# Moving the first batch's small work inside its periods: squares, narrowing of w_in, low part of x, hops of the sums

## The chip, the cores and the metric

The kernel runs on one core of one Trainium2 chip, as a single launch. The metric is device time in microseconds (us); smaller is better. Three runs of the kernel before gave 1159.63, 1160.09 and 1160.9 us, so its median is 1160.09 us.

## The reference

Three stages follow one another. Attention: q, k, v are 4 batches x 12 heads x 448 rows x 64; q and k are divided by the root mean square of their rows, then softmax and the product with v. An MLP on the 1792 tokens of 768 features. A mixture of 8 experts with a fixed capacity of 224 tokens each.

```
q_n, k_n = rmsnorm(q, g_q), rmsnorm(k, g_k)          # x / sqrt(mean(x*x) + 1e-6) * g
scores = q_n @ k_n.T / 8;  attn = softmax(scores);  x = attn @ v
h = x @ w_in;  g = h * clip(h + 3, 0, 6) / 6;  x = g @ w_out      # 768 -> 2048 -> 768
logits = x @ w_gate          # greedy assignment, largest logits first, 224 tokens per expert
out[mask_e] = relu(x[mask_e] @ w1[e]) @ w2[e]
```

w_in and w_out arrive as 64-bit floats, seen as pairs of 32-bit words; the kernel narrows them to 32-bit floats itself.

## The kernel before

Attention works on pairs of heads: pair i has two heads of one batch, six pairs make a batch, 24 pairs in all. For each pair: `load` (L229) brings q and k (224 KB each); `squares` (L251, ScalarE, "ACT") squares them; for pairs 2 to 9 `fold` (L256, GpSimd, "POOL") adds halves of the squares; `sums` (L267, VectorE, "DVE") reduces them; `guess` (L271, L272, DVE) makes a first value of the inverse root; `invert` refines it in three Newton steps (12 small instructions, L279 to L282, on POOL for pairs 1 to 9); `norm` (L298, POOL) multiplies q and k by it into xn; `transp` (L315) transposes xn on TensorE ("PE"), and L324 (ACT) and L327 (DVE) split the result into a high and a low part, qh, ql, kh, kl. `s1` (L338) makes scores, whose maxima DVE takes (mx, L341); `mt` (L347) transposes the maxima, and L349 (DVE) makes mr of them. `sT` (L360) makes the transposed scores less their maxima, ACT takes the exponentials (ph, L371). `pv` (L449) multiplies by v and L452 (ACT) copies the result into xn_t, of which there are two buffers. `psums` (L460 or L465) adds up the exponentials.

The sums then take a way through DRAM, called the hops here: `rs_out` (L471) stores them, `rs_in` (L476) loads them in another shape (rs), `rec` (L482, L483, DVE) takes the reciprocal (rr), `r_out` (L487) stores it, `r_in` (L493) loads it spread over the partitions (rb). `xmul` (L497, POOL) multiplies xn_t by rb, and `xsplit` makes the high part xh (L507, ACT) and the low part xl (L505, POOL). xl is the last reader of an xn_t buffer.

Beside this runs the narrowing of w_in, 16 units: a load of 768 KB (wraw, L159), one ACT and three DVE instructions (cv, L141 to L144) and a store of 384 KB (L174). From the end of the first batch the MLP of the batch that is done (h, L559) fills PE between the pieces of attention. Its weights w are loaded from the narrowed ones (win_v, L181), split by ACT and POOL or DVE (L118, L119) into one of three buffers, and stored for later batches (w_hl, L545, 768 KB).

All engines follow an order written out by hand. Each step of pair i has a due time on a scale on which a pair takes 16 units: `at(t + T, fn, i)`, with t = 16 i. The events are sorted by due time and each instruction is put at the end of its engine's queue; no engine takes one ahead of another. SyncE ("SP") issues all these DMAs in one such queue: a hop that waits for the DMA before it holds up everything behind it.

Of the kernel before, what the change touches and what calls it, by code (L numbers as in the profile page):

```python
# [21 lines left out]
def kernel(  # L22
# [45 lines left out]
    CI, CI0, CI1, CI2, CO = 6, 1.75, 2.5, 0.5, 1.5  # L68

    T_LOAD, T_VLOAD, T_NORM, T_Q, T_K, T_V = -72, -12, -38, -30, -28, 6  # L70
    T_SUMS, T_INV, T_INV0, NG0 = -50, -42, -35.5, 10
    T_S1, T_MT = (-24, -23.9, -16, -15.9), -9
    T_ST = (0, 0.1, 8, 8.1)
    T_AV = ((17, 18, 19.5, 20.5), (22, 23, 24.5, 25.5))
    T_NUM, T_XT, T_MLP = 28, 33, (37, 41, 41, 37)
    T_ADD, T_PV, T_SUM = (6, 13), (15.6, 15.62, 15.64, 15.66), 15.7
    T_RS, T_RL, T_REC, T_RO, T_RB, T_X, T_XH, T_XL = 19.5, 21.5, 24, 25.5, 28, 33, 35.5, 39.5
    GD, WD2, C_ST = 12, 8, 5
    TX0 = (20, 23, 27, 29, 32.5, 39, 42, 46)
    QMAJOR = (NP - 1, B * NP - 1)  # L80
    T_CI, D_CI, T_CO, D_CO, T_CL = 20, 10, 180, 12, 14


    order = ExitStack()
# [652 lines left out]
    def at(t, fn, *args):  # L737
        events.append((t, len(events), fn, args))
# [6 lines left out]

    for i in range(NH // 2):
        t = 16 * i
        at(t + T_LOAD, load, i)
        at(t + T_VLOAD, vload, i)
        g = GROUP[i]  # L750
        first = 16 * g[0]
        t_sq = first + T_SUMS + 4 * (i - g[0])
        at(t_sq, squares, i)
        if 2 <= i < NG0:
            at(t_sq + 2, fold, i)
            t_sq += 3
        at(t_sq, sums, i)
        late_g = 4 <= g[0] < NG0
        if i == g[-1]:
            at(t_sq if 2 <= i < NG0 else first + T_INV, guess, g)  # L760
            at(first + (T_INV0 if late_g else T_INV), invert, g)
        at(t + (T_INV0 + 0.1 if late_g and i == g[0] else T_NORM), norm, i)
        at(t + T_Q, transp, i, 0)
        at(t + T_K, transp, i, 1)
        at(t + T_V, vsplit, i)
        for c in range(NCH):
            at(t + (T_S1[c] if i else -24 + 0.1 * c), s1, i, c)
            at(t + (T_ST[c] if i else (-9, -8.9, 1, 1.1)[c]), sT, i, c)
            if i in QMAJOR:
                for s in range(2):  # L770
                    at(t + T_AV[s][c], av, i, s, c)
            else:
                at(t + T_PV[c], pv, i, c)
        at(t + (T_MT if i else -21), mt, i)
        if i in QMAJOR:
            at(t + T_NUM, normalize, i)
            at(t + T_XT, xt, i)
        else:
            for n in range(2 if i >= NP else 0):
                at(t + T_ADD[n], padd, i, n)  # L780
            at(t + T_SUM, psums, i)
            tx = TX0 if i < NP else (T_RS, T_RL, T_REC, T_RO, T_RB, T_X, T_XH, T_XL)
            for d, fn in zip(tx, (rs_out, rs_in, rec, r_out, r_in, xmul)):
                at(t + d, fn, i)
            at(t + tx[6], xsplit, i, False)
            at(t + tx[7], xsplit, i, True)
        if (i + 1) % NP == 0:
            at(t + T_MLP[i // NP], mlp_next, i // NP)
# [1 line left out]
    at(8 * H + 2, prefetch, 0)  # L790
    at(8 * H + 14, prefetch)
    for u in range(NF if wide else 0):
        for out_, t in ((0, T_CI + D_CI * u), (1, T_CO + D_CO * u)):
            at(t - T_CL, conv, (out_, u), -1)
            for part in (0, 1, 2, 3, C_ST):
                at(t + part, conv, (out_, u), part)
# [446 lines left out]
    for pi, (t, hfs) in enumerate(passes):  # L1243
# [10 lines left out]
        for f in range(NF):  # L1254
            i, k = divmod(f, QF)
# [139 lines left out]
```

## Time and profile before

| | |
|---|---|
| median of three runs | 1160.09 us |
| profiled execution: time, span of the core | 1162.06 us, 1160.2 us |
| PE busy | 1099.2 us, 95% of the span |
| DVE busy | 692.2 us, 60% |
| ACT busy | 521.3 us, 45% |
| POOL busy | 464.6 us, 40% |
| DMA | 232.17 MB, mean 200 GB/s |

The span runs from the first to the last instruction; 1.86 us of the profiled time lie outside it. The page cuts the span into 40 slices of 29 us. PE is at nine tenths or more in nearly all of them; the slices below that are mainly the first seven, and the granted clock of PE (full is 2.4 GHz, the other level 1.2 GHz) is below full mainly in slices 3, 4 and 6. A "period" in what follows is the time from one transpose of the maxima (PE t L347, one in each pair) to the next. In the first batch one takes between 12 and 20 us.

### The profile page before, as it was taken

Reading aid. Unit: us, or ns where it says so; the run is one execution under the profiler, and the core shown is the slowest. Engines: PE = TensorE matmul, PEld = TensorE weight load, DVE = VectorE, ACT = ScalarE, POOL = GpSimd, SP = SyncE. Lnnn points to the kernel's source line nnn. Section 1 sums busy time; section 2 is a strip of 40 time slices with the busy share of each in tenths; the row PEclk is TensorE's granted clock in tenths of the full one; section 3 lists DMA queues with packets and bytes.
Section 4 is the critical chain, followed back from the end, with each engine's and each line's share of the span. In section 5 each row is a group of like instructions: output and inputs, shape, how many; then the busy total and the mean of one; then the engine's idle time right before and its main releaser. Section 6 shows DMA issues by size and latency. Waiting matters only on the chain.

```text
span 1160.2 us, 19232 instructions
## 1 busy us (share of the span) xinstructions
PE 1099.2 (95%) x7073; PEld 880.7 (76%) x7073; DVE 692.2 (60%) x1440; ACT 521.3 (45%) x941; POOL 464.6 (40%) x410
## 2 busy tenths in 40 slices
PE   4978899999999999999999999999997999999997
PEld 3446556766766667787767888888887899999997
DVE  7877877886677845212341666666665846555550
ACT  4655555745545556533542111111114766666551
POOL 4665555664445533112444000000004677775540
PEclk9987989999999999999999999999998999999999
DMA  4575998978777887659996222222237888877731
GB/s 133 145 197 148 248 300 252 309 238 297 251 250 253 257 288 239 222 190 276 356 310 204 78 69 82 64 76 71 70 104 185 245 262 247 248 227 217 226 130 39
DMA packets 215357, 232.17 MB, mean 200 GB/s; under 512 B 28296, under 2 KB 188384, under 8 KB 215264
## 3 DMA queue, kind: packets, MB, share of 16 engines
q1 hardware_dynamic: 211936, 219.94, 61.6%
q0 software_dynamic: 3328, 11.01, 3.1%
q8 instruction: 55, 0.90, 0.3%
q14 instruction: 38, 0.31, 0.1%
HBM read 179.82 MB, written 51.09 MB: 199 GB/s over the span
## 4 chain that ended last, share of the span: by engine, by line
PE 67%; DVE 10%; DMA 9%; issue 5%; POOL 4%; ACT 3%; SPq 1%; POOLq 0%; DVEq 0%; ACTq 0%
PE y L1195 19%; PE h L559 15%; PE y L1347 8%; PE h L1283 5%; PE st L360 4%; PE av L449 4%; PE h L1285 3%; DMA w_hl<-w 2%; DMA we_s<-in_moe_w_dram 2%; DVE mx L341 2%; PE rt L988 1%; PE lg L601 1%; PE sm L465 1%; DMA gr<-g_dr 1%; DVE cv L143 1%
## 5 line engine op out<-in xcount | busy, mean ns | idle before, releaser
L559 PE MATMUL h<-xh,w 128*128 128x448 f32 x768 | 239.9, 382 | 1.0 <-DVE mx L341 0.5
L559 PEld LDWEIGHTS h<-xh,w 128*128 128x128 f32 x768 | 143.3, 191 | 35.9 <-issue 22.1
L559 PE MATMUL h<-xl,w 128*128 128x448 f32 x384 | 145.7, 379 | 0.0
L341 DVE TENSOR_REDUCE mx<-s 112x1 f32<-112x448 f32 x192 | 105.9, 611 | 51.6 <-PE s L338 51.3
L1133 ACT ACTIVATE g2h<-gr 128x512 fp32r<-128x512 f32 x60 | 37.9, 631 | 206.1 <-PE y L1195 161.6
L1195 PE MATMUL y<-woh,g2l 128*128 128x512 f32 (+1 forms) x448 | 124.8, 344 | 1.0 <-POOL g2l L1098 1.0
L1195 PE MATMUL y<-woh,g2h 128*128 128x512 f32 (+1 forms) x448 | 125.3, 345 | 0.0
L1195 PE MATMUL y<-wol,g2h 128*128 128x512 f32 (+1 forms) x448 | 125.2, 344 | 0.0
L1098 POOL TENSOR_TENSOR g2l<-gr,g2h 128x512 fp32r<-128x512 f32 x14 | 19.0, 1361 | 240.6 <-DMA gr<-g_dr 209.0
L119 POOL TENSOR_TENSOR wel<-we_s,weh 128x768 fp32r<-128x768 f32 x48 | 96.3, 2010 | 45.4 <-ACT weh L118 37.0
L118 ACT ACTIVATE weh<-we_s 128x768 fp32r<-128x768 f32 x107 | 88.4, 841 | 57.9 <-DMA we_s<-in_moe_w_dram 39.3
L119 DVE TENSOR_TENSOR wel<-we_s,weh 128x768 fp32r<-128x768 f32 x59 | 78.3, 1334 | 60.3 <-ACT weh L118 53.6
L371 ACT ACTIVATE ph<-st 112x448 f32<-112x448 f32 x192 | 93.0, 545 | 40.8 <-PE st L360 39.7
L442 POOL TENSOR_TENSOR pa<-ph 112x448 f32<-112x448 f32 x68 | 85.6, 1279 | 44.2 <-ACT ph L371 44.2
L1283 PE MATMUL h<-xe,weh 128*128 128x448 f32 x318 | 100.4, 375 | 2.0 <-DVE xe L1234 2.0
L559 PEld LDWEIGHTS h<-xl,w 128*128 128x128 f32 x384 | 73.2, 191 | 11.9 <-issue 7.0
L1195 PEld LDWEIGHTS y<-woh,g2l 128*128 128x128 f32 x448 | 72.0, 189 | 10.7 <-POOL g2l L1098 1.3
L1195 PEld LDWEIGHTS y<-woh,g2h 128*128 128x128 f32 x448 | 71.9, 189 | 10.6 <-issue 1.5
L1195 PEld LDWEIGHTS y<-wol,g2h 128*128 128x128 f32 x448 | 71.9, 189 | 9.1 <-issue 0.7
L1285 PE MATMUL h<-xe,wel 128*128 128x224 f32 x318 | 76.6, 268 | 0.0
L562 ACT ACTIVATE r<-h,half 128x448 f32<-128x448 f32 x64 | 40.6, 634 | 77.7 <-PE h L559 67.3
L497 POOL TENSOR_TENSOR xn_t<-xn_t,rb 128x448 f32<-128x448 f32 x22 | 25.8, 1175 | 119.7 <-DMA rb<-rec_dr 119.7
(252 smaller groups left out, 2386.1 us busy)
## 6 DMA issues: line engine op xcount, KB each, us to landing
we_s<-in_moe_w_dram SPq DMA_DIRECT2D x128, 384.0 KB
w<-w_hl SPq DMA_DIRECT2D x32, 768.0 KB
gr<-g_dr SPq DMA_DIRECT2D x52, 256.0 KB
wraw<-in_moe_w_in_dram SPq DMA_DIRECT2D x16, 768.0 KB
win_v<-w SPq DMA_DIRECT2D x32, 384.0 KB
w_hl<-w SPq DMA_DIRECT2D x16, 768.0 KB
wraw<-in_moe_w_out_dram SPq DMA_DIRECT2D x16, 768.0 KB
g_dr<-g SPq DMA_DIRECT2D x48, 224.0 KB
```

The lines of the kernel that those rows point to most:

```text
L118: nc.scalar.activation(hi, raw, AF.Copy)
L119: eng.tensor_tensor(lo, raw, hi.bitcast(F32), op=OP.subtract)
L341: mx = nc.vector.tensor_reduce(MX[i][:, s, c:c + 1], pp[s][:CP, :S], axis=AX.X, op=OP.max)
L360: nc.tensor.matmul(pp[s][:CP, :S], a[r], b[r], start=(n == 0), stop=(n == len(todo) - 1))
L371: nc.scalar.activation(e, pp[s][:CP, :S], AF.Exp)
L442: nc.gpsimd.tensor_tensor(PA[i, s, n], PP[i, s, 2 * n][0], PP[i, s, 2 * n + 1][0], op=OP.add)
L449: nc.tensor.matmul(p[r, :S], vvs[i % 2][:, s, c, V0:V0 + 64], PP[i, s, c][0], start=(c == 0), stop=(c == NCH - 1))
L559: nc.tensor.matmul(p[:, :S], lhs[:, c], x[:, c], start=(n == 0), stop=(n == 3 * NC - 1))
L1195: nc.tensor.matmul(pp[hf][:, :COLS[hf].stop - COLS[hf].start], a[:, f % QF], w[:, COLS[hf]], start=(f == 0 and n == 0), stop=(f == NF - 1 ...
L1283: mm = [lambda: nc.tensor.matmul(p[:, :4 * CP], wh[:, fo], x.rearrange("d k t -> d (k t)"), start=(c == 0), stop=(c == NC - 1), skip_group ...
L1285: lambda: nc.tensor.matmul(p[:, :2 * CP], wl[:, fo], x[:, 0], start=False, stop=False, skip_group_check=True)]
L1347: nc.tensor.matmul(p[:CP, :HW], a[:, f, tk], w[:, o], start=(f == 0 and n == 0), stop=(f == FB - 1 and n == 2))
```

## The change

Only due times change, for the first batch mostly. The squares of pairs 4 to 9 come one pair in each period, behind kh, instead of two in every other period. Their sums and folds go with them. The narrowing of w_in comes at hand-picked times, one unit in each odd period and two in each even one, behind the first four maxima; before it came every 10 units of due time whatever stood there. Its stores come 8.5 behind its start instead of 5, its loads 12.5 ahead instead of 14 (both also for w_out). The q and k loads of pairs 4 and up come 4 later. In the hops of the first batch the store of the sums comes 1.5 earlier, the load and the reciprocal 0.5 earlier, the load of rb 0.5 later, the multiplication 1.3 later, and the low part 2 earlier.

```diff
-    T_SUMS, T_INV, T_INV0, NG0 = -50, -42, -35.5, 10
+    T_SUMS, T_SQ, T_INV, T_INV0, NG0 = -50, -58.9, -42, -35.5, 10
-    GD, WD2, C_ST = 12, 8, 5
-    TX0 = (20, 23, 27, 29, 32.5, 39, 42, 46)
+    GD, WD2, C_ST = 12, 8, 8.5
+    TX0 = (18.5, 22.5, 26.5, 28.5, 33, 40.3, 42, 44)
-    T_CI, D_CI, T_CO, D_CO, T_CL = 20, 10, 180, 12, 14
+    T_CO, D_CO, T_CL = 180, 12, 12.5
+    T_CI = [16 * i + t for i in range(1, 11) for t in ((8.3, 12.3) if i % 2 == 0 or i > 6 else (8.3,))]
...
-        at(t + T_LOAD, load, i)
+        at(t + (T_LOAD if i < 4 else -68), load, i)
...
-        t_sq = first + T_SUMS + 4 * (i - g[0])
+        late_g = 4 <= g[0] < NG0
+        t_sq = t + T_SQ if late_g else first + T_SUMS + 4 * (i - g[0])
...
-        for out_, t in ((0, T_CI + D_CI * u), (1, T_CO + D_CO * u)):
+        for out_, t in ((0, T_CI[u]), (1, T_CO + D_CO * u)):
```

The change adds one line near the top, so that a line of the kernel before stands one lower in the changed one.

On DVE, around the end of the fourth period (q and k of pair 7), the kernel before has:

```order
L142 TENSOR_SCALAR cv<-cv 128x768
L327 SCALAR_TENSOR_TENSOR ql<-t,gq_72,qh 128x448
L143 SCALAR_TENSOR_TENSOR cv<-wraw,cv 128x768
L144 SCALAR_TENSOR_TENSOR cv<-wraw,cv 128x768
L327 SCALAR_TENSOR_TENSOR kl<-t,gk,kh 128x448
L267 TENSOR_REDUCE st_2_1240<-sq 112x8 x2
L271 TENSOR_SCALAR st_2_1240<-st_2_1240 112x32
L272 TENSOR_SCALAR st_2_1241<-st_2_1240 112x32
L349 TENSOR_TENSOR mr<-t,place 128x448
```

At the same place the changed kernel has:

```order
L145 SCALAR_TENSOR_TENSOR cv<-wraw,cv 128x768
L342 TENSOR_REDUCE mx_128<-s_1211 112x1
L342 TENSOR_REDUCE mx_128<-s_1212 112x1
L342 TENSOR_REDUCE mx_128<-s_1231 112x1
L342 TENSOR_REDUCE mx_128<-s_1232 112x1
L328 SCALAR_TENSOR_TENSOR ql<-t,gq_72,qh 128x448
L328 SCALAR_TENSOR_TENSOR kl<-t,gk,kh 128x448
L350 TENSOR_TENSOR mr<-t,place 128x448
```

Nothing stands between ql, kl and mr any more; the narrowing has gone ahead of the last four maxima of the period.

On ACT, at the same pair's high parts, the kernel before has:

```order
L141 ACTIVATE cv<-wraw 128x768
L371 ACTIVATE ph<-st 112x448 x2
L324 ACTIVATE qh<-t,gq_72 128x448
L251 ACTIVATE sq<-ld_q 112x512
L251 ACTIVATE sq<-ld_k 112x512
L324 ACTIVATE kh<-t,gk 128x448
```

and the changed kernel:

```order
L372 ACTIVATE ph<-st 112x448 x4
L325 ACTIVATE qh<-t,gq_72 128x448
L325 ACTIVATE kh<-t,gk 128x448
L252 ACTIVATE sq<-ld_q 112x512
L252 ACTIVATE sq<-ld_k 112x512
```

The squares have gone behind kh.

On POOL, in the third period, the kernel before has the multiplication, the first Newton step of pairs 6 and 7, then (eleven steps on) xn of pair 6 and the low part:

```order
L497 TENSOR_TENSOR xn_t<-xn_t,rb 128x448
L279 TENSOR_TENSOR st_2_885<-st_2_884 112x32
...
L298 TENSOR_TENSOR xn_998<-ld_q,st_2_884 112x2x4x64
L298 TENSOR_TENSOR xn_1000<-ld_k,st_2_884 112x2x4x64
L505 TENSOR_TENSOR xl<-xn_t,xh 128x448
```

and the changed kernel:

```order
L498 TENSOR_TENSOR xn_t<-xn_t,rb 128x448
L506 TENSOR_TENSOR xl<-xn_t,xh 128x448
L280 TENSOR_TENSOR st_2_787<-st_2_786 112x32
...
L299 TENSOR_TENSOR xn_996<-ld_q,st_2_786 112x2x4x64
L299 TENSOR_TENSOR xn_998<-ld_k,st_2_786 112x2x4x64
```

The low part has gone ahead of the twelve Newton instructions and of xn.

## Rows read from the trace of the kernel before

**Rows 1.** Busy time by period: stretch, length, PE, PEld, DVE, ACT, POOL, clock, DMA, GB/s.

```profile
37.53:51.19 13.66, 11.37 (x81) 5.82 (x81) 11.88 (x25) 10.27 (x20) 8.31 (x16) 1.00 0.43 123
51.19:64.42 13.23, 11.39 (x82) 6.04 (x82) 11.88 (x18) 7.59 (x16) 6.66 (x6) 1.00 0.71 185
64.42:82.90 18.48, 14.24 (x81) 7.02 (x82) 12.74 (x25) 8.68 (x17) 11.49 (x19) 0.82 0.72 198
82.90:95.27 12.37, 12.00 (x83) 6.42 (x81) 9.31 (x17) 9.70 (x19) 5.78 (x6) 0.86 0.73 211
95.27:115.43 20.16, 16.97 (x98) 14.07 (x98) 15.79 (x26) 9.90 (x19) 11.78 (x20) 0.72 0.46 124
115.43:135.59 20.16, 17.85 (x104) 10.77 (x104) 15.77 (x24) 12.11 (x24) 10.24 (x8) 0.86 0.96 244
157.87:184.56 26.69, 23.29 (x120) 15.92 (x118) 19.58 (x28) 12.99 (x24) 12.27 (x9) 0.87 0.96 300
```

**Rows 2.** Timeline of ACT, third period: start, length, what, idle before and releaser.

```profile
80.41 0.54 ACT L452 ACTIVATE xn_t<-av 128x448 f32<-128x448 f32 x1 [7.31 <-POOL xl L505]
```

**Rows 3.** Timeline of POOL, third period.

```profile
69.93 1.77 POOL L497 TENSOR_TENSOR xn_t<-xn_t,rb 128x448 f32<-128x448 f32 x1 [3.10 <-DMA rb<-rec_dr]
71.67 0.23 POOL L279 TENSOR_TENSOR st<-st 112x32 f32<-112x32 f32 x1
...
79.25 1.13 POOL L505 TENSOR_TENSOR xl<-xn_t,xh 128x448 fp32r<-128x448 f32 x1
```

**Rows 4.** Timeline of DVE, fifth period.

```profile
99.44 0.67 DVE L327 SCALAR_TENSOR_TENSOR kl<-t,gk,kh 128x448 fp32r<-128x448 f32 x1
...
101.60 0.18 DVE L272 TENSOR_SCALAR st<-st 112x32 int32<-112x32 int32 x1
...
108.59 0.28 DVE L482 TENSOR_TENSOR rr<-rs 112x8 f32<-112x8 f32 x1 [4.16 <-DMA rs<-sum_dr]
```

**Rows 5.** Timeline of PE: fifth and sixth period, and one wait later on.

```profile
111.02 4.61 PE L400 MATMUL av<-vv,ph 112*112 112x66 f32 x24
...
127.08 2.79 PE L465 MATMUL sm<-pa,ones 112*32 112x448 f32 x4 [2.16 <-POOL pa L442]
...
162.82 0.71 PE L360 MATMUL st<-qh,kh 64*112 64x448 f32 x1 [2.68 <-DVE g L564]
```

**Rows 6.** Groups of DVE instructions, 37.53 to 115.43: busy us, mean ns | idle before.

```profile
L143 DVE SCALAR_TENSOR_TENSOR cv<-wraw,cv 128x768 int32<-128x768 int32 x8 | 10.7, 1334 | 0.1
L144 DVE SCALAR_TENSOR_TENSOR cv<-wraw,cv 128x768 int32<-128x768 int32 x8 | 8.4, 1049 | 0.1
L142 DVE TENSOR_SCALAR cv<-cv 128x768 int32<-128x768 int32 x8 | 5.1, 640 | 1.1 <-ACT cv L141 1.1
```

**Rows 7.** Timeline of POOL: first period's Newton steps, fifth period's, the sixth's multiplication.

```profile
41.38 0.48 POOL L279 TENSOR_TENSOR st<-st 112x32 f32<-112x32 f32 x1 [1.43 <-DVE st L272]
...
46.59 0.54 POOL L282 TENSOR_TENSOR st<-st,st 112x32 f32<-112x32 f32 x1
...
101.86 0.24 POOL L279 TENSOR_TENSOR st<-st 112x32 f32<-112x32 f32 x1 [0.33 <-DVE st L272]
...
105.72 1.04 POOL L298 TENSOR_TENSOR xn<-ld_q,st 112x512 f32<-112x512 f32 x1
...
121.77 1.13 POOL L497 TENSOR_TENSOR xn_t<-xn_t,rb 128x448 f32<-128x448 f32 x1 [10.43 <-DMA rb<-rec_dr]
```

**Rows 8.** SP's queue: loads of rb for pairs 7 and 17, first and last of six.

```profile
173.73 1.11 SPq L493 DMA_DIRECT2D rb<-rec_dr  x2
...
387.04 1.10 SPq L493 DMA_DIRECT2D rb<-rec_dr  x2
```

**Rows 9.** Timeline of ACT: squares of q of pairs 13 and 23.

```profile
182.15 0.63 ACT L251 ACTIVATE sq<-ld_q 112x512 f32<-112x512 f32 x1
...
394.42 0.62 ACT L251 ACTIVATE sq<-ld_q 112x512 f32<-112x512 f32 x1
```

**Rows 10.** Chain of waits: the longest transfer it holds from 140 to 260.

```profile
241.20 9.68 DMA w_hl<-w
```

More of the change, by code (lines that the diff above doesn't have):

```diff
@@ L757 @@
         at(t_sq, sums, i)
-        late_g = 4 <= g[0] < NG0
         if i == g[-1]:
```

## The prediction

> **What bounds the kernel now.** I read the page's slices first: PE is busy 95% of the span, and where it is not, and where its clock is below full, is mainly the first 180 us. So I cut the first batch into periods, from one transpose of the maxima to the next, and read busy time and granted clock of each [rows 1]. From 51 to 136 us these take 13.23, 18.48, 12.37, 20.16 and 20.16 us (the second to the sixth; the first took 13.66). PE is idle for 1.8, 4.2, 0.4, 3.2 and 2.3 us in them, and the clock is 0.82, 0.86, 0.72 and 0.86 of full in the last four. There are only two levels, 1.2 and 2.4 GHz, so 0.72 over 20.16 us means 11.3 us at the lower one, which costs up to 5.6 us in that period. The drops come behind waits.
>
> Then I looked for what PE waits for. In the third period ACT stood 7.31 us ahead of the copy into xn_t, until POOL had made the low part xl of an earlier pair, the last reader of that buffer [rows 2]. POOL had its multiplication from 69.93 on, then the Newton steps of the next two pairs from 71.67, then their xn, and xl only at 79.25 [rows 3]: 9.3 us from the start of the multiplication to xl, most of it work of other pairs. In the fifth period DVE has a whole narrowing between ql and kl: kl comes at 99.44, the guess at 101.60, 6.3 us into the period; then it waits 4.16 us for the sums, until 108.59 [rows 4]. Behind that late reciprocal rb is late too, and POOL stands 10.43 us in the sixth period [rows 7], for which PE waits 2.16 us with the sums of the exponentials [rows 5]. These are stages in which short waits on several engines in turn set the pace, and not PE.
>
> **The change part by part.** No instruction is added or taken away; they change places. I go by periods, in the profiled execution's time.
>
> *First and second period.* The first has no late part of x in it; I take no change. In the second, DVE now has two narrowings. One is 1.33 + 1.05 + 0.64 = 3.0 us [rows 6]. DVE's busy time in the first five periods is 61.6 us, of which eight narrowings are 24.2; the rest is 7.5 us a period. So a period with one narrowing needs 10.5 us of DVE and one with two needs 13.5. The second took 13.23: +0.3. The fourth took 12.37, with 9.31 us of DVE [rows 1]: +1.1. Here DVE becomes the bound, since the last four maxima now stand behind both narrowings. At best the instructions overlap a little and both stay as they are (0); at worst the reciprocal ahead of the second narrowing waits for its sums as it did in the fifth period, 4.16 us each (+8).
>
> *Third period.* The low part goes ahead of the Newton steps, so the copy into xn_t no longer waits for them. What is late next is the Newton steps themselves, and xn behind them, which PE's transposes of the next pair need. The guess comes 6.3 us into a period as before [rows 4] (four maxima are put ahead of it, a narrowing is taken from there). xl takes 1.13 [rows 3], part of it beside the wait for the guess: Newton starts at 6.8. The twelve steps took 3.9 us beside maxima only (101.86 to 105.72), and 5.75 beside a narrowing (41.38 to 47.13), where a single step took 0.48 instead of 0.24 [rows 7]. Now a narrowing follows the guess, so I take 5, the nearer to the second: 11.8. Two xn of 1.04 each: 13.9, and half a microsecond for the last transposes (an estimate): 14.4 against 18.48, -4.1. Ends: 12.4, as the fourth period has it now, is -6.1; no gain at all is 0, where rb lands as late as now.
>
> The Trainium skill (SBUF — State Buffer, Who interferes with whom) has a rule that speaks against this place: a DVE instruction with two SBUF inputs, or in a 2-port mode, and a GpSimd instruction that reads SBUF lock each other out, and the second waits for the whole of the first. By it the Newton steps would be longer by all three narrowing instructions, 3.9 + 3.0 = 6.9, and the gain of each of the two periods 1.9 us less; the trace's 5.75 shows less than that.
>
> *Fifth period.* ql, kl and mr follow each other with nothing between, and kh is no longer behind the squares. The reciprocal no longer stands behind a load of 768 KB issued between the store of the sums and their load. What is late next is again xn, at 13.9. Behind its transposes stand 24 small products that took 4.61 us at the low clock [rows 5]; at full speed half. So 13.9 + 0.5 + 2.3 to 4.6 is 16.7 to 19; I take 17, as the waits ahead of the clock's fall are gone: -3.2. Ends: 0, and PE's busy 16.97 less the 5.6 of the clock plus 3.2 of idle time, 14.6, -5.6.
>
> *Sixth period.* With the reciprocal some 6 us earlier in the fifth, rb lands that much earlier and of POOL's 10.43 us most goes: PE's 2.16 us go, and some of the clock's loss (0.86 over 20.16 is 5.6 us at the low level, 2.8 us): -3. Ends: -5 and 0.
>
> *The later loads and stores.* By the start of the MLP's first unit one unit of w_in less has been loaded and stored: 1152 KB come into a stretch that already moves 300 GB/s with the DMA at 0.96 [rows 1], 3.8 us of transfer. PE is idle there for 3.4 us of 26.69, so part of this shows: +2, from 0 to +4. All later stages keep their order on PE, so I cost them at nothing; what hides the later q and k loads is the time between their issue and their squares (third rival).
>
> Sum: 0.3 + 1.1 - 4.1 - 3.2 - 3 + 2 = -6.9 us. The profiled execution took 1162.06 us (span 1160.2 and 1.86 around it), and would take 1155.2; it lies 2 us above the median of 1160.09. The same difference from the median gives 1153. With the ends of the likely terms, -6.1 to 0 and so on, this case has a range of its own of 1148 to 1157.5.
>
> **The rivals.** *The clock stays up.* If no wait of the new order is long enough to lower it, all the low-clock time of the third to sixth period (3.3, 1.7, 5.6 and 2.8 us of loss) goes and the idle time of the third and fifth with it: about -14, 1146. For it: each fall follows waits that the change removes. Against: PE still waits for xn in odd periods and for the maxima in even ones.
>
> *The hops stay late, and the weights' stretch takes the rest.* rb still lands late, since the multiplication is ahead of xl and the Newton steps on POOL, and the two narrowings hold up the reciprocal. The third and fifth period then gain some 2 us each, the fourth loses 1.1, the sixth gains nothing, and 2 to 4 us go to the transfers: -0.5, 1159.6. For it: 3.10 and 10.43 us of waiting for rb [rows 3, 7]. Against: the load of rs now goes ahead of wraw, and there is more time for each hop.
>
> *Slower: late q and k in the later batches.* The loads of pairs 13, 15 to 23 move behind the load of rb. Their squares stand between qh and kh on ACT. From the issue of rb's end to the squares are 182.15 - 174.84 = 7.3 us for pair 13 and 394.42 - 388.14 = 6.3 for pair 23 [rows 8, 9], six pairs of this kind. If q and k land as late as the slowest weight store here, 9.68 us [rows 10], squares and kh are 2.4 to 3.4 us late. With about 1.3 us of slack behind kh (an estimate) PE waits for 1.1 to 2.1 us in each, some 9 us, and if half of these waits lower the clock as the one of 2.68 us at 162.82 did [rows 5] (0.87 over 26.69 us is 3.5 us of loss [rows 1]), another 10: -7 + 19 = +12, 1172; it outweighs the gain from a landing of about 8.5 us on. For it: the DMA is at 0.96 in the stretch of pair 13 [rows 1]. Against: q and k together are 448 KB, little more than half of that store.
>
> **How the numbers follow.** The forecast has 0.56, the clock that stays up 0.17, late hops 0.15, late q and k 0.12. A measurement of this kernel can tell about 0.2% from no change, 2.3 us, so faster is below 1157.8. The first case gives 0.53 of its chance to faster and 0.03 to no change, the second all to faster, late hops 0.04 to faster, 0.09 to no change and 0.02 to slower: 0.74 faster, 0.12 no change, 0.14 slower. The range reaches down past the second case's 1146 and up to the late hops with somewhat more transfer time: 1145 to 1162.
>
> **What would show it.** Right: third and fifth period near 14.4 and 17 us; no wait of ACT for xl over 2 us; Newton steps the last thing ahead of PE's transposes; even periods of 13 to 14 us with the maxima as PE's releaser; POOL's 10.43 us mostly gone; all later stretches of the same length within some us. Wrong: if POOL still waits for rb in the third and fifth period by over 3 us; if PE waits for kh in the later batches, or ACT's squares for ld_q; or if the stretch from the first MLP unit to 235 us is longer by more than 4 us.

## The result, and the profile after

The changed kernel takes 1175.26 us (median of four runs, 1173.16 to 1178.29), the kernel before beside it 1160.49 us: a ratio of 1.0118, 95% interval 1.0076 to 1.016. It is slower by some 14 us. The profiled execution of the changed kernel is the longest of its four, 1178.29 us with a span of 1176.5 us.

Busy time by period after the change, where [rows 1] stood (stretch, length, then PE, PEld, DVE, ACT, POOL, clock, DMA share, GB/s):

```profile
40.72:54.07 13.35, 10.64 (x82) 5.79 (x82) 9.89 (x21) 8.44 (x17) 8.14 (x16) 1.00 0.69 184
54.07:68.05 13.98, 11.96 (x84) 6.70 (x82) 12.71 (x22) 10.33 (x19) 5.87 (x6) 0.88 0.37 104
68.05:84.72 16.67, 12.86 (x81) 7.54 (x82) 11.50 (x21) 8.44 (x16) 9.90 (x18) 0.81 0.89 236
84.72:98.91 14.19, 12.18 (x83) 6.84 (x81) 12.73 (x22) 10.30 (x19) 5.77 (x6) 0.86 0.38 105
98.91:121.64 22.73, 15.63 (x97) 14.09 (x98) 12.13 (x23) 8.76 (x17) 14.35 (x23) 0.65 0.88 232
121.64:141.60 19.96, 17.34 (x104) 10.65 (x104) 16.91 (x22) 12.13 (x23) 9.41 (x6) 0.89 0.53 134
```

Against before the first to sixth period are -0.31, +0.75, -1.81, +1.82, +2.57 and -0.20 us; ahead of the first 3.2 us are lost, from 141.6 to 457 us another 8.4, and 1.9 after that. That is 16.3 us, the difference of the two spans. In the fifth period PE is idle for 7.1 us and its clock is 0.65.

PE's waits in the changed kernel (start, length, what, idle before and releaser), the first ahead of the first period, then those at the ends of the second, third and fourth, all of the fifth with what followed, and two in the sixth:

```profile
30.71 4.87 PE L450 MATMUL av<-ph,vv 112*64 112x448 f32 x16 [0.89 <-ACT vv L305]
...
68.05 0.35 PE L348 MATMUL t<-ident,mx 112*128 112x112 f32 x1 [2.02 <-DVE mx L342]
82.92 2.01 PE L316 MATMUL t<-ident,xn 112*128 112x112 f32 x8 [3.81 <-POOL xn L299]
98.91 0.45 PE L348 MATMUL t<-ident,mx 112*128 112x112 f32 x1 [2.01 <-DVE mx L342]
...
107.77 2.04 PE L401 MATMUL av<-vv,ph 112*112 112x66 f32 x16 [2.63 <-ACT ph L372]
114.27 1.01 PE L316 MATMUL t<-ident,xn 112*128 112x112 f32 x4 [4.46 <-POOL xn L299]
115.07 1.63 PE L401 MATMUL av<-vv,ph 112*112 112x66 f32 x8
116.49 0.95 PE L316 MATMUL t<-ident,xn 112*128 112x112 f32 x4
117.24 4.61 PE L401 MATMUL av<-vv,ph 112*112 112x66 f32 x24
121.64 0.39 PE L348 MATMUL t<-ident,mx 112*128 112x112 f32 x1
...
133.58 0.94 PE L466 MATMUL sm<-pa,ones 112*32 112x448 f32 x2 [1.69 <-POOL pa L443]
135.46 0.94 PE L466 MATMUL sm<-pa,ones 112*32 112x448 f32 x2 [0.94 <-POOL pa L443]
```

The even periods wait for the maxima, as forecast; the odd ones wait for xn, and from the first xn in the fifth to its end 7.4 us pass. The other wait of the fifth, 2.63 us for ph, has the same origin as the late xn: on ACT these exponentials stand behind xh, and xh waits for rb and the multiplication.

POOL in the fifth period, where [rows 7] stood, and its next two waits:

```profile
105.22 1.45 POOL L498 TENSOR_TENSOR xn_t<-xn_t,rb 128x448 f32<-128x448 f32 x1 [2.79 <-DMA rb<-rec_dr]
107.36 1.13 POOL L506 TENSOR_TENSOR xl<-xn_t,xh 128x448 fp32r<-128x448 f32 x1 [0.69 <-ACT xh L508]
108.45 0.24 POOL L280 TENSOR_TENSOR st<-st 112x32 f32<-112x32 f32 x1
108.77 0.25 POOL L281 TENSOR_TENSOR st<-st,st 112x32 f32<-112x32 f32 x1
109.11 1.08 POOL L282 TENSOR_SCALAR st<-st 112x32 f32<-112x32 f32 x1
...
113.17 1.04 POOL L299 TENSOR_TENSOR xn<-ld_q,st 112x512 f32<-112x512 f32 x1
...
119.21 1.13 POOL L498 TENSOR_TENSOR xn_t<-xn_t,rb 128x448 f32<-128x448 f32 x1 [1.82 <-DMA rb<-rec_dr]
...
129.21 1.91 POOL L506 TENSOR_TENSOR xl<-xn_t,xh 128x448 fp32r<-128x448 f32 x1 [6.86 <-ACT xh L508]
```

DVE in the same period, where [rows 4] stood:

```profile
105.04 0.18 DVE L273 TENSOR_SCALAR st<-st 112x32 int32<-112x32 int32 x1
...
108.89 0.17 DVE L483 TENSOR_TENSOR rr<-rs 112x8 f32<-112x8 f32 x1 [1.40 <-DMA rs<-sum_dr]
...
109.21 0.91 DVE L145 SCALAR_TENSOR_TENSOR cv<-wraw,cv 128x768 int32<-128x768 int32 x1
```

The guess is 6.1 us into the period, as forecast (6.3). But the Newton steps begin at 9.5, behind rb, the multiplication, ACT's xh and xl.

In the later batches the squares [rows 9] now wait for q on ACT at two pairs, 13 and 17, and what that does shows on DVE and PE. First ACT and PE at pair 13, then ACT, DVE, POOL and PE at pair 17:

```profile
191.14 0.63 ACT L252 ACTIVATE sq<-ld_q 112x512 f32<-112x512 f32 x1 [2.16 <-DMA ld_q<-in_q_dram]
194.41 0.46 PE L339 MATMUL s<-kh,qh 64*112 64x448 f32 x2 [1.25 <-ACT kh L325]
...
279.47 0.63 ACT L252 ACTIVATE sq<-ld_q 112x512 f32<-112x512 f32 x1 [0.99 <-DMA ld_q<-in_q_dram]
...
280.14 1.28 DVE L268 TENSOR_REDUCE st<-sq 112x8 f32<-112x512 f32 x2 [0.94 <-ACT sq L252]
...
282.14 1.16 POOL L506 TENSOR_TENSOR xl<-xn_t,xh 128x448 fp32r<-128x448 f32 x1
282.30 1.03 DVE L272 TENSOR_SCALAR st<-st 112x32 f32<-112x32 f32 x1
...
286.17 0.47 PE L560 MATMUL h<-xh,w 128*128 128x448 f32 x1 [2.05 <-DVE mr L350]
```

SP's queue ahead of pair 17, which answers [rows 8]: the load of rb, then q, 7.75 us before its squares could start.

```profile
269.45 2.23 SPq L494 DMA_DIRECT2D rb<-rec_dr  x2
271.72 0.66 SPq L230 DMA_DIRECT2D ld_q<-in_q_dram  x1
```

In the kernel before, the same load was issued ahead of the store of the reciprocal, 3.4 us into its period; now it is issued 12.4 us into it, 9.0 us later:

```profile
251.78 0.46 SPq L229 DMA_DIRECT2D ld_q<-in_q_dram  x1
```

The stretch that follows (same columns as the first table; the kernel before first) is 3.45 us longer, with the clock at 0.93 instead of 1.00:

```profile
271.46:292.81 21.35, 21.24 (x128) 15.27 (x127) 13.89 (x32) 10.77 (x20) 10.22 (x10) 1.00 0.79 257
280.91:305.71 24.80, 22.75 (x127) 16.61 (x126) 15.15 (x33) 11.72 (x22) 12.13 (x12) 0.93 0.84 277
```

### The profile page after: what moved, and what is told of

The parts are those of the page before. It is cut to its first block, busy times and chain, and to the rows that moved or that the text cites. A ratio compares the mean times of both kernels' runs of the same rounds, so it can differ in the third digit from the quotient of the medians.

```text
span 1176.5 us, 19196 instructions
## 1 busy us (share of the span) xinstructions
PE 1101.2 (94%) x7073; PEld 885.3 (75%) x7073; DVE 689.9 (59%) x1440; ACT 522.0 (44%) x941; POOL 461.6 (39%) x410
## 4 chain that ended last, share of the span: by engine, by line
PE 65%; DMA 11%; DVE 11%; issue 5%; ACT 3%; POOL 2%; SPq 2%; POOLq 0%; DVEq 0%; ACTq 0%
PE y L1196 19%; PE h L560 14%; PE y L1348 8%; PE h L1284 5%; PE av L450 4%; PE st L361 3%; PE h L1286 3%; DMA sum_dr<-rb 2%; DMA rec_dr<-rr 2%; DVE mx L342 1%; DMA we_s<-in_moe_w_dram 1%; PE rt L989 1%; PE lg L602 1%; DMA gr<-g_dr 1%; DVE cv L144 1%
## 5 line engine op out<-in xcount | busy, mean ns | idle before, releaser
L1196 PEld LDWEIGHTS y<-woh,g2h 128*128 128x128 f32 x448 | 72.0, 189 | 10.6 <-issue 1.5
L450 PE MATMUL av<-ph,vv 112*64 112x448 f32 x352 | 72.7, 556 | 1.0 <-ACT vv L305 0.9
```

The costliest lines, as they stand in the source:

```text
L450: nc.tensor.matmul(p[r, :S], vvs[i % 2][:, s, c, V0:V0 + 64], PP[i, s, c][0], start=(c == 0), stop=(c == NCH - 1))
L1196: nc.tensor.matmul(pp[hf][:, :COLS[hf].stop - COLS[hf].start], a[:, f % QF], w[:, COLS[hf]], start=(f == 0 and n == 0), stop=(f == NF - 1 ...
```

## The experiments

The theories after the result: L, the late q and k loads; S, the squares; N, the narrowing; H, the hops. All ratios are to the kernel before, run beside each, with a 95% interval. "Change of period" is against the kernel before, each from one profiled execution.

**One part taken back.** From the changed kernel, one of these each:

```diff
# late loads back
-        at(t + (T_LOAD if i < 4 else -68), load, i)
+        at(t + T_LOAD, load, i)
# squares back
-        t_sq = t + T_SQ if late_g else first + T_SUMS + 4 * (i - g[0])
+        t_sq = first + T_SUMS + 4 * (i - g[0])
# narrowing back
-    T_CI = [16 * i + t for i in range(1, 11) for t in ((8.3, 12.3) if i % 2 == 0 or i > 6 else (8.3,))]
+    T_CI = [20 + 10 * u for u in range(16)]      # and C_ST = 5, T_CL = 14
# hops back
+    TX0 = (20, 23, 27, 29, 32.5, 39, 42, 46)
```

Loads back. 

> The changed kernel with the q and k loads of all pairs back at -72 (4 earlier); all else as changed. Theory L (the loads are late): in the trace of the changed kernel ACT's squares wait for ld_q 3 times, 5.6 us, and POOL, DVE and PE stand behind that; the fifth period (22.73 us) comes back to 20 or less, the stretch from 141.6 to 352.2 us, which is 8.3 us longer than before, shrinks by 4 to 8, and the time falls from 1175 to some 1164 to 1168. Theory S (place of the squares and the narrowing on ACT and DVE): the waits for ld_q go and something else ends last; 1172 to 1176.

1167.57 us, 1.0053 (1.0034 to 1.0072): more than half of the loss is gone. ACT waits for ld_q nowhere after the first 10 us of the kernel. But the fifth period is still 21.3 us.

Squares back. 

> The changed kernel with the squares, folds and sums of pairs 4 to 9 back at their old places (two pairs in every other period, ahead of kh). Theory S: PE's wait for vv of pair 0 and its 4.87 us of products at the lower clock go (first period 12.42 back to 9.9 from 27.7 on, -2.6), the fifth period too; 1169 to 1171. Theory L: with the loads still late the squares of the odd pairs now come 3.1 earlier on the scale than in the changed kernel, so they wait longer for ld_q and the time does not fall or rises: 1174 to 1180.

1175.32 us, 1.0112 (1.0084 to 1.0139): no gain, as L expected. The loss ahead of the first period goes (0.0 instead of +2.57), the second period grows (+2.73).

Narrowing back. 

> The changed kernel with the narrowing as before: one unit every 10, stores at 5, loads at 14 ahead, for w_in and w_out. Theory N (two narrowings in a period and the later transfers are what costs): the even periods, 13.98 and 14.19 us, go back to 13.2 and 12.4 (-2.6), the reciprocal's waits for rs (17.0 us in nine) shrink, the stretch up to 352 us falls by 5 or more: 1164 to 1168. Theories L and S: -3 at most, 1171 to 1176.

1176.13 us, 1.01 (1.0066 to 1.0133): N alone isn't it. The even periods do go back (-0.8, +0.6), but the first becomes 3.87 us longer.

Hops back. 

> The changed kernel with the old due times of the hops, the low part again behind the Newton steps and xn. If the hops are the part that gains (third period 18.48 to 16.67), it is slower by 2 to 6: 1177 to 1181. If the wider hops are what costs (the multiplication 1.3 later holds xn_t and POOL), it is faster by 3 to 6: 1169 to 1172.

1175.69 us, 1.0112 (1.0081 to 1.0143): the hops neither gain nor cost. The third period loses its gain (+0.80 instead of -1.81), as a part that gains would show, and other periods make up for it.

**Which late loads, and two parts at a time.** The first two are the changed kernel with `-68` only for i >= 10, and only for 4 <= i < 10:

```diff
+        at(t + (T_LOAD if i < 10 else -68), load, i)
# and
+        at(t + (-68 if 4 <= i < 10 else T_LOAD), load, i)
```

Late for pairs 10 and up. 

> The changed kernel with the q and k loads 4 later for pairs 10 and up only; pairs 4 to 9 are loaded as before. With no late load the time was 1167.6 us, with all late 1175.3. Theory A (the rival of the prediction: in the later batches q and k come behind r_out and the load of rb on SP, and squares and kh are late): most of the 7.7 us comes back, 1173 to 1176. Theory B (first batch: q and k come behind a load of wraw of 768 KB on SP, and the squares of pairs 5 to 9 with POOL's fold behind them are late): 1167 to 1169, and the stretch from 142 us on is as long as with no late load.

1174.75 us, 1.012 (1.0105 to 1.0134): theory A, all of it.

Late for pairs 4 to 9. 

> The changed kernel with the q and k loads 4 later for pairs 4 to 9 only; pairs 10 and up are loaded as before. Theory A: 1167 to 1170. Theory B: 1172 to 1176, ACT waits for ld_q in the fifth period as in the changed kernel (2.46 us).

1169.01 us, 1.0075 (1.0062 to 1.0088): within the spread of the kernels here without a late load (1.0051 to 1.0095).

The other two take back two parts of the changed kernel, loads and squares, or loads and narrowing (the lines above together). Hops and narrowing kept:

> The kernel before with the hops and the narrowing of the change, but the squares and the loads of before. With squares, narrowing and hops it was 1167.6, some 6 us above before. If the squares are what is left (vv of pair 0 behind them, +1.2 in the first period; POOL's fold waits 19 us for them), this is at 1160 to 1163 or below; if the narrowing in twos is (even periods +1.0 and +1.9), it stays at 1165 to 1168.

1167.92 us, 1.0069 (1.0054 to 1.0084): no gain over all three, so taking the squares out does not help while hops and narrowing stay.

Hops and squares kept:

> The kernel before with the squares and the hops of the change, but the narrowing and the loads of before. If the narrowing in twos is what is left, this is at 1160 to 1163 or below, with even periods of 13.2 and 12.4 us; if the squares are, it stays at 1164 to 1168 with the first period 1 to 3 us longer.

1171.2 us, 1.0095 (1.0065 to 1.0125): nor does taking the narrowing out; the first period is +3.86, as with the narrowing back.

**One part alone.** Each is the kernel before with the lines of the change for that part only: `TX0`; `T_CI`, `C_ST` and `T_CL`; `T_SQ` and `t_sq`; and squares with narrowing.

```diff
# hops alone, against before
-    TX0 = (20, 23, 27, 29, 32.5, 39, 42, 46)
+    TX0 = (18.5, 22.5, 26.5, 28.5, 33, 40.3, 42, 44)
# narrowing alone, against before (and T_CI as in the change)
-    GD, WD2, C_ST = 12, 8, 5
+    GD, WD2, C_ST = 12, 8, 8.5
-    T_CI, D_CI, T_CO, D_CO, T_CL = 20, 10, 180, 12, 14
+    T_CO, D_CO, T_CL = 180, 12, 12.5
# squares alone, against before
-        t_sq = first + T_SUMS + 4 * (i - g[0])
+        t_sq = t + T_SQ if late_g else first + T_SUMS + 4 * (i - g[0])
```

> The kernel before with the hops' due times of the change alone (low part ahead of the Newton steps). All three kernels that keep the hops and drop the late loads are 6 to 10 us above before. Theory H (the hops are the common cost: POOL's low part waits for xh and the Newton steps and xn stand behind it): 1165 to 1168, with the fifth period of 21 us or more. Theory N (the hops gain 2 to 4 us as forecast and the narrowing or the squares lose more): 1156 to 1160, third period below 16 us.

1162.36 us, 1.0023 (1.0004 to 1.0041): theory H falls. But the hops don't gain either: the third period is 17.4 us, not below 16.

> The kernel before with the narrowing of the change alone (units in odd and even periods by hand, stores at 8.5, loads at 12.5 ahead). Theory N: 1165 to 1169, even periods +2.7 and +1.8 with PE waiting for the maxima. Theory H: 1160 to 1163.

1163.15 us, 1.0023 (1.0007 to 1.0039): N falls as the common cost, though the even periods are +1.68 and +2.57 as it said; the first, third and fifth gain.

> The kernel before with the squares of the change alone (pairs 4 to 9, behind kh, one pair in each period). First period +1 to +2.6, as vv of pair 0 stands behind the squares on ACT; the fifth may gain the 1.0 us that PE waits for kh. Either theory: 1160 to 1164. Above 1166 the squares would be the common cost instead (POOL stands up to 6 us at the fold, with rb's multiplication behind it).

1169.91 us, 1.0079 (1.006 to 1.0099): the squares cost most by themselves. PE in the first period of this kernel, and POOL's first Newton step ahead of that, 8.2 us into the period instead of 3.9 [rows 7]:

```profile
54.42 2.01 PE L316 MATMUL t<-ident,xn 112*128 112x112 f32 x8 [4.56 <-POOL xn L299]
```

```profile
46.89 0.24 POOL L280 TENSOR_TENSOR st<-st 112x32 f32<-112x32 f32 x1 [4.11 <-DVE rr L483]
```

The squares of the second pair now start 3.1 later on the scale, its sums and the guess fall behind four maxima on DVE, and Newton, xn and PE's transposes follow. The three kernels with the new squares and the old narrowing all show it (+3.86, +3.86, +3.87); with the new narrowing, which leaves that place, it is -0.3.

> The kernel before with the squares and the narrowing of the change, but the hops and the loads of before. Theory H: 1160 to 1163. Theory N: 1166 to 1171, as much as with the hops or more, since the third period keeps its wait for the low part.

1168.36 us, 1.0071 (1.0045 to 1.0097): N's number, but N has fallen alone; two parts together cost more than either theory's one.

**What was still open.**

```diff
# loads of pairs 10 and up behind r_out only, against the changed kernel
+        at(t + (T_LOAD if i < 10 else -70), load, i)
# squares behind vv (and all loads as before), against the changed kernel
+    T_SUMS, T_SQ, T_INV, T_INV0, NG0 = -50, -57.9, -42, -35.5, 10
# all work later, against before
-    at(T_LOAD, load_scales)
+    at(T_LOAD - 1, load_scales)
# a smaller dose, against before
+            at(t + (44 if i == 1 else tx[7]), xsplit, i, True)
+        t_sq = first + T_SUMS + (6.1 if 4 <= g[0] < NG0 else 4) * (i - g[0])
```

> The changed kernel with the q and k loads of pairs 4 to 9 as before and those of pairs 10 and up 2 later instead of 4: on SP they then stand behind the store of the reciprocal (r_out), but ahead of the load of rb, which waits for that store. Theory R (the load of rb in front of q and k is what makes them late): close to no late load, 1167 to 1170. Theory S (r_out in front of them is enough, since it waits for DVE's reciprocal): 1172 to 1176, as with 4.

1174.65 us, 1.0099 (1.0072 to 1.0125): r_out in front is enough, by the time. But here ACT waits for q nowhere in the later batches. In the period from 253.4 to 276.5 us rb, issued 10.1 us in, is used by POOL at 20.8, and in the next one, issued at 8.3, at 15.5; in the kernel with the loads back the two are 10.1 and 18.9, 10.4 and 14.1. So rb takes 1.9 and 3.5 us longer with q and k issued just ahead of it; by the completion signals in the two traces it lands 10.6 and 7.1 us after its issue, instead of 8.6 and 3.6. The one place of its trace that costs 3 us lies between, on POOL, DVE and PE:

```profile
277.49 1.14 POOL L506 TENSOR_TENSOR xl<-xn_t,xh 128x448 fp32r<-128x448 f32 x1
```

```profile
277.60 1.08 DVE L273 TENSOR_SCALAR st<-st 112x32 int32<-112x32 int32 x1
```

```profile
281.31 0.47 PE L560 MATMUL h<-xh,w 128*128 128x448 f32 x1 [1.59 <-DVE mr L350]
```

Again mr is late and PE waits, here since rb, xh and kh came later and the guess met xl. That rb lands late is shown; that q and k are the reason is inferred from these numbers.

> The changed kernel with all loads as before and the squares of pairs 4 to 9 one step later, behind vv instead of ahead of it. If PE's wait for vv behind the squares (0.9 us in the first period, with the clock's fall behind it up to 2.6) is what the squares cost, 1163 to 1166 against 1167.6; if the later squares, and the guess and xn behind them, are, 1167 to 1171.

1167.96 us, 1.0051 (1.0032 to 1.0069): as with the squares ahead of vv. The loss ahead of the first period goes (0.0), and the whole doesn't follow.

> The kernel before with the four small loads of the scales ahead of the first q and k on SP, so that all work begins some 1.5 us later in the same order. If the falls of the clock hang on the waits alone, +1 to +2.5 us (1162 to 1164). If they hang on when a wait comes as well, as two kernels suggest that wait 0.89 and 0.90 us for vv and of which one loses the clock (0.69) and the other doesn't (1.00), the periods of the first batch change by 1 to 4 us each in either direction, and the time by up to 6.

1163.88 us, 1.0007 (0.9991 to 1.0024): the time moves as if by the waits alone. But its periods, with the same order, change by -2.8 to +1.6 us each, as the other reading has it, and the sum cancels.

> The kernel before with two parts of the change in a smaller dose: the low part ahead of the Newton steps for pair 1 alone (third period, where ACT stood 7.31 us for it; not in the fifth, where it costs 2.3), and the squares of pairs 5, 7 and 9 behind kh but ahead of vv. PE's waits for kh (1.50, 1.00 us) go; the guess comes some 1 us later. 1156 to 1160 if that is a gain, 1161 to 1164 if the later guess and xn take it back.

1161.45 us, 0.9986 (0.9966 to 1.0006): perhaps 1 us better, not told apart from the kernel before.

**The other side.** From the kernel before, and from the smaller dose:

```diff
-        at(t + T_LOAD, load, i)
+        at(t + (T_LOAD if i < 10 else -76), load, i)
```

> The kernel before with the q and k loads of pairs 10 and up 4 earlier (-76) and nothing else. With r_out ahead of q and k the load of rb has 448 KB just ahead of it and lands some 3 us later in the fourteenth and fifteenth period; with rb ahead of them q and k are late. Theory C (q and k and the hops hurt each other when they are close): more distance gains too, 1155 to 1159. Theory M (there is a margin that is only used up behind r_out): no change, 1160 to 1163.

1163.91 us, 1.0019 (1.0002 to 1.0037). 

> The kernel before with the smaller dose of the change (low part ahead of the Newton steps for pair 1 alone, squares of pairs 5, 7 and 9 behind kh) and the q and k loads of pairs 10 and up 4 earlier. The smaller dose alone was 0.9986 of before. Theory C: 1153 to 1158. Theory M: 1158 to 1161.

1164.68 us, 1.0023 (1.0004 to 1.0041): theory C falls; earlier loads gain nothing. No version here beats the kernel before by more than can be told.

**The late loads, over the kernels.** Growth against the kernel before from 135.6 to 442.7 us of it, in us, beside the median:

| kernel | late loads, pairs 10 up | 135.6 to 442.7 | median |
|---|---|---|---|
| changed | yes | +8.4 | 1175.3 |
| squares back | yes | +8.6 | 1175.3 |
| narrowing back | yes | +4.3 | 1176.1 |
| hops back | yes | +4.0 | 1175.7 |
| late for 10 up only | yes | +6.9 | 1174.8 |
| behind r_out only | half | +5.4 | 1174.7 |
| loads back | no | +2.1 | 1167.6 |
| late for 4 to 9 only | no | 0.0 | 1169.0 |
| hops, narrowing | no | +0.4 | 1167.9 |
| hops, squares | no | +1.5 | 1171.2 |
| squares, narrowing | no | +0.7 | 1168.4 |
| squares behind vv | no | +0.7 | 1168.0 |
| squares alone | no | +0.8 | 1169.9 |
| hops alone | no | -2.9 | 1162.4 |
| narrowing alone | no | -3.1 | 1163.2 |

Six kernels with them lie at 1174.7 to 1176.1, and the seven without that have the squares or more than one part at 1167.6 to 1171.2, 6.4 us apart in the mean; the traces have 5.4 us of that in the stretch where the loads are (+6.3 against +0.9). Against the kernel before run beside each the distance is smaller: the ratios are 1.0110 and 1.0070 in the mean, 0.4% or 4.6 us. Four pairs of kernels differ in the late loads alone, with all parts, without the squares, without the narrowing and without the hops: 1.0118 and 1.0053, 1.0112 and 1.0069, 1.01 and 1.0095, 1.0112 and 1.0071. All four point the same way; the third is within its intervals. So the late loads cost some 5 to 7 us.

How they cost it differs from kernel to kernel. ACT's wait for q at pair 17 is in three of the six traces (changed, squares back, hops back). With the loads late for 10 up only, and with the narrowing back, the stretch behind pair 17 grows by 0.1 us or less, and 2.8 us of the growth lie in the last period of the stretch, where PE waits 1.75 and 1.77 us for the maxima. The kernel with hops and squares, which has no late load, has a period like that too (+2.66, PE waits 1.54 us for DVE's g).

## Why the prediction was wrong

The forecast was -6.9 us; between the two profiled executions the span grew by 16.3. Ahead of the first period 0 was forecast and 3.2 measured, for the first six periods -8.9 and +2.8, for all that follows +2 and +10.3.

*Later loads and stores, +2.* This is the step with the largest error. It took the later q and k loads at nothing, with "the time between their issue and their squares" to hide them. They cost some 5 to 7 us; the stretch from 141.6 us on, with what follows, is 10.3 longer. The +2 itself, for the narrowing's later transfers, does not show: with the narrowing alone that stretch is 3.1 shorter than before. The rival on late q and k had the right cause, with a chance of 0.12. That its time, 1172, is near the measured one is luck: it added 19 us for the loads to a gain of 7, and the runs have 5 to 7 for the loads and a loss of some 6 for the rest. Its mechanism was right up to ACT: squares wait 2.16 and 0.99 us for q, against the 2.4 to 3.4 it gave. Only at pair 13 does kh carry it to PE, as it said, with 1.25 us there. At pair 17 it goes through sums, guess and DVE's Newton steps to mr, which stand in a row on DVE, and PE waits 2.05 us for mr, with 1.7 us of clock loss behind it (0.07 of 24.80). The rival against it, that q and k are "little more than half" of a slow weight store, weighed size, where the distance in SP's queue decided: q of pair 17 was issued 9.0 us later in its period, and 7.75 us were left to its squares.

*First period, "no change".* The period itself is (-0.31). But the stretch just ahead of it, which the sum left out, lost 2.6 us: the squares of pair 4 went ahead of vv on ACT, and PE waited 0.89 us for vv and ran the products at the lower clock, 4.87 us. An edit was looked at where it was meant to act, and not at the first pair it reaches.

*Second and fourth period, +0.3 and +1.1.* Right in mechanism: PE waits 2.02 and 2.01 us for the maxima behind two narrowings; the size was +0.75 and +1.82.

*Third period, -4.1.* Half came: -1.81. ACT's wait for xl is gone (1.26 us is left of 7.31 [rows 2]). "Newton starts at 6.8" failed: it started at 8.6, since rb was used at 5.7, and xl stood behind it with ACT's xh in between. The guess was no longer the last to arrive.

*Fifth period, -3.2.* Wrong in sign, +2.57, by two errors. The first is the same: rb at 6.3, Newton at 9.5 instead of 6.8, and the first xn done at 15.3 instead of 12.8. With the loads back these are 5.1, 8.1 and 13.9, so 1.4 us of the late xn go with the late loads (in the changed kernel ACT stands 2.46 us for q, until 100.3 us), and the rest comes from the order on POOL. The second was in the reading: behind the first transposes stand 8 products, four more transposes and 24 products, 7.4 us with the granted clock at 0.50, not the 24 alone. In the kernel before PE took those transposes without any wait 12.84 us into the period:

```profile
108.11 0.95 PE L315 MATMUL t<-ident,xn 112*128 112x112 f32 x4
108.86 1.63 PE L400 MATMUL av<-vv,ph 112*112 112x66 f32 x8
110.28 0.95 PE L315 MATMUL t<-ident,xn 112*128 112x112 f32 x4
```

From there to the end of the period, in the kernel before and the changed one (columns as in the first table):

```profile
108.11:115.43 7.32, 7.32 (x43) 7.32 (x42) 6.74 (x10) 2.06 (x3) 3.23 (x3) 0.50 0.21 54
114.27:121.64 7.37, 7.37 (x40) 7.37 (x41) 1.59 (x3) 2.17 (x4) 5.55 (x6) 0.50 0.97 267
```

So with the forecast's own 12.8 for the first xn the period comes to 20.2 us, as before, and only a higher clock could shorten it. The changed order made xn late instead.

The rule of the Trainium skill weighed there (SBUF — State Buffer, Who interferes with whom) holds for single instructions: one Newton step took 1.08 us instead of 0.24 and ended with the DVE instruction of 0.91 beside it. But not all three narrowing instructions met the steps: one did in the fifth period, where they took 4.7 us, and two in the third, the first of them with its end only, where they took 5.2. That is near the 5 taken and not the 6.9 worked out with all three.

*Sixth period, -3.* POOL's 10.43 us for rb are gone, as forecast, and nothing was gained (-0.20): POOL stood 6.86 us at xl for ACT's xh, and PE waited 1.69 and 0.94 us for the sums of exponentials where it had waited 2.16. The wait was replaced.

*The rival of a clock that stays up.* It did not come: the clock was 0.81 to 0.89 in four of the periods and 0.65 in the fifth. Its sum was also short: the 13.4 us of clock loss that it lists and 7.4 us of idle time are 20.8, not 14.

*What stays open.* Without the late loads the change still costs 0.5%, some 6 us, and its parts don't add up: 2.7 us for hops or narrowing alone, 9 for the squares, 6 for all three. Part of it is shown: the squares' 3.9 us hang on where the narrowing stands. Many periods between 95 and 190 us change by 1 to 6 us from kernel to kernel, in both directions, and one by 2.8 us when all work is shifted by 1.6 us. Why loads behind r_out alone cost as much as behind both hops is shown at one place only, and where the late loads' cost arises in the two kernels without ACT's wait at pair 17 is not shown.

## What to carry to other kernels

A load that moves past a hop is late by the hop's whole wait (here 9.0 us for a move of a quarter of a period), so measure its distance to its user in the queue that issues it, for every pair it moves and not for the stage that the change is about. When a wait is removed, list what else the same instruction needs and take the last of them, and compare the result with when its user wanted it before: if the user did not wait, nothing is to be gained there. On an in-order engine small steps that move behind four maxima or a narrowing are late by all of those, so parts of a schedule have to be tried together and apart.

## What the runs showed of the hardware

The same wait does not always cost the clock. In the changed kernel and in the one with the loads back PE waits 0.89 and 0.90 us for vv ahead of the same 16 products. In the first they take 4.87 us, in the second 3.23; PE there:

```profile
30.39 3.23 PE L450 MATMUL av<-ph,vv 112*64 112x448 f32 x16 [0.90 <-ACT vv L305]
```

The stretch from 31 to 36 us, first of the changed kernel, then of that with the loads back (columns as in the first table): the clock is 0.69 in one and 1.00 in the other.

```profile
31.00:36.00 5.00, 5.00 (x24) 1.48 (x25) 3.01 (x7) 0.37 (x1) 4.50 (x11) 0.69 0.02 5
```

```profile
31.00:36.00 5.00, 5.00 (x38) 1.87 (x36) 3.12 (x7) 1.18 (x2) 4.48 (x11) 1.00 0.15 52
```

So a period in one trace can be 1.6 us longer with the same order of work in it, and small terms are better read from several kernels. And DVE's short instructions are held by POOL as well: each of the guess's two instructions takes 0.17 to 0.18 us by itself, and one of them took 1.03 and 1.08 us beside a low part of 1.16 and 1.14 us on POOL, and ended within 0.05 us of it (at 282.30 in the changed kernel, and at 277.60 in the kernel with the loads behind r_out only).
